# Weights of the first two experts asked for later, in an attention and mixture-of-experts kernel

## The chip, the cores and the metric

The kernel runs on one core of one Trainium2 chip, as one launch. The metric is device time in microseconds (us). TensorE (PE), VectorE (DVE), ScalarE (ACT) and GpSimd (POOL) each work through a list of instructions of their own, in order; SyncE (SP) issues most DMAs, GpSimd issues the indirect ones (gather and scatter by an index) and a few others. An instruction waits at the head of its engine's list until what it needs is there, and all that stands behind it waits too.

## What is computed

A gated linear attention over 4 sequences of 768 tokens with 8 heads of 40, and a mixture of 16 experts on its rows (3072 tokens, 320 wide, hidden size 1024). Cut to what matters:

```python
for t in range(S):                                   # attention, state C and n per sequence and head
    m_new = maximum(f[t] + m, i[t]); fs = exp(f[t] + m - m_new); is_ = exp(i[t] - m_new); m = m_new
    C = fs * C + is_ * outer(v[t], k[t]);  n = fs * n + is_ * k[t]
    y[t] = sigmoid(o[t]) * (C @ q[t]) / maximum(abs(n @ q[t]), 1)
x = y as rows of 320 (8 heads x 40)
g = argmax(x @ w_group)                              # one of 4 groups, then one of 4 experts in it
e = argmax(x @ w_expert[g])
out = softmax(..)[g] * softmax(..)[e] * (relu(x @ w1[g, e]) @ w2[g, e])
```

## The kernel before

**Attention.** The sequence is cut into 6 chunks of 128 tokens; a chunk of one of the 4 sequences is a unit, so there are 24 units, 0 to 23. A unit multiplies keys and queries (`sp`, line 200), weighs them with decays (`pt`, 205), adds what the carried state gives (`si`, 225) and multiplies with the values (`av`, 266). Its inputs are four kinds of DMA on SP: `ab` (the decays, 512 KB), `qk` (two of 192 KB), `nt` (values and keys, 324 KB), and every fourth unit `sig`. `ab` and `qk` of a unit are asked for four units ahead, `nt` three units ahead. Two units ahead GpSimd masks `ab` (`affine_select`, line 160) and ScalarE takes its exponential (190). For units below 20 GpSimd also scales the output rows (`hn`, 288), behind the mask in its list. The rows of the unit before (`x`, 293) are written to `x_d` in DRAM (301), transposed on TensorE (306) and multiplied with the routing weights (`lg`, 327).

**Routing.** `route()` (line 333 on) turns four units' logits into slots of an index table `itab` in DRAM. It is a generator: each small step, one to three instructions, is taken by `go_on()`, of which a unit has five; `go_on(7)` behind units 13 to 15 takes seven more. For the last two chunks it runs in two parts, over three units and over one. GpSimd scatters a unit's token numbers to `itab` (`put_id`, 455). At unit 13 `first_experts()` is put in the same list: from the counts so far it picks the two experts that go first, and its last steps put 8 tasks in `early_loads` (each asks for half of `w1`, 768 KB, or half of `w2`, 640 KB: for the first expert w1, w1, w2, w2, and then the same for the second) and 7 tasks in `early_splits`.

**Splits.** Weights are used as a sum of two rounded parts. A split task casts a piece on ScalarE (609) and lists the subtraction that gives the low part for VectorE (611, `lows`). The first expert has seven: w1, w1, a third piece `wsk`, and four quarters of w2.

**The turn from attention to experts.** Behind unit 22, when chunks 0 to 4 are routed, the last slots are scattered, the first expert's index list is read back (`ix`, 581), and 256 rows are gathered from `x_d` in two gathers (`xg`, 548). They are transposed (`tpm`, 646), split by ScalarE and VectorE (`xhl`, 653 and 654), and `expert((0, 0), 256)` starts (`psh`, 725; `po`, 758 to 760). Rows of the last chunk that belong to this expert come with a second, late gather of 128 rows. The other 15 experts follow one after the other, each with its weights loaded two experts ahead.

**What sets the order.** Units 2 to 21 are written out in the order in which they run (`manual_schedule`). From unit 22 on a planner places the instructions by its own costs; `issue_after` holds a block behind a given instruction and `high_priority` brings it forward. The stretch that the change touches:

```python
for u in range(2, MANUAL):                                     # MANUAL = 22
    unit(u)
    go_on(7 if 13 <= u <= 15 else 0)
    do(early_loads, 1 if 14 <= u < 20 else 0)
    do(lows)
    do(early_splits, {16: 1, 17: 1, 18: 2, 20: 2, 21: 1}.get(u, 0))
```

so that six halves are asked for behind units 14 to 19, one behind each, and the last two behind the last unit's write to `x_d`.

Of the kernel before, what the change touches and what calls it, by code (L numbers as in the profile page):

```python
# [7 lines left out]
F32 = mybir.dt.float32  # L8
# [4 lines left out]
ALU = mybir.AluOpType  # L13
# [5 lines left out]
P = 128  # L19
# [34 lines left out]
def bc(ap, shape):  # L54
    return ap.broadcast_to(list(shape))
# [3 lines left out]
def lstm_moe(ctx: ExitStack, tc: tile.TileContext, gates, qkT, nat, og, wcat, w1, w2, cst, out):  # L59
    nc = tc.nc  # L60
# [59 lines left out]
    rt = {"manual": True}  # L120


    def busy(n):
        t = ps_s.tile([P, 512], F32, name="busy", tag="sp")
        for _ in range(n):
            mm(t, ones_b, bc(ones_b.unsqueeze(1), (P, 4, P)), start=True, stop=True)
# [288 lines left out]
    def go_on(n=1):  # L415
        for _ in range(n):
            if chores:
                with ExitStack() as st:
                    if not rt["manual"]:
                        st.enter_context(tc.high_priority())  # L420
                    if next(chores[0], StopIteration) is StopIteration:
                        chores.pop(0)
# [28 lines left out]
    def put_id():  # L451
        if ids:
            sl, tk = ids.pop(0)
            nc.gpsimd.memset(sep, 0.0)
            no_order("ids", nc.gpsimd.indirect_dma_start(
                out=itab_flat, out_offset=bass.IndirectOffsetOnAxis(ap=sl, axis=0), in_=tk, in_offset=None))
# [120 lines left out]
    def load_ix(r, q=None):  # L577
        nb = len(blocks(CAPS[r]))
        ixs[r] = mxp.tile([P, 3, 2], I32, name="ix", bufs=5)
        t = itab[0:NE * NBLK].rearrange("(e n) p o -> e n p o", e=NE)  # L580
        (q or nc.sync).dma_start(ixs[r][:, 0:nb], t[bass.ds(ereg[r], 1), 0:nb].rearrange("o n p i -> p (o n) i"))

    def blocks(W):
        return [min(P, W - i) for i in range(0, W, P)]
# [15 lines left out]
    lows = []  # L600
# [33 lines left out]
    def turn_tasks(key, W, xg, banks=None):  # L634
        t = {}

        def one(i, m):
            if i == 0:
                pool = pools["xhl"][len(xhls) % len(pools["xhl"])]
                sh, dt = ([P, 3, W], F32) if key[0] in FULL else ([P, 3, 2, W], F32R)  # L640
                t["x"] = xhls[key] = pool.tile(sh, dt, name="xhl", bufs=1)
            xhl, g = t["x"], xg[i]
            pool, tag = (banks or ((ps_1, "tp"), (pools.get("ps_t"), "tg"), (ps_1, "av")))[i]
            tp = pool.tile([P, 3, P], F32, name="tpm", tag=tag)
            for k in range(3):
                nc.tensor.transpose(out=tp[:, k, :], in_=g[:, k * P:(k + 1) * P], identity=ident)  # L646
            if key[0] in FULL:
                nc.scalar.copy(xhl[:, :, i * P:i * P + m], tp[:, :, 0:m])

                nc.vector.memset(xhl[DM - 2 * P:, 2, i * P:i * P + m], 0.0)  # L650
                return
            xh = xhl[:, :, 0, i * P:i * P + m]
            nc.scalar.copy(xh, tp[:, :, 0:m])  # L653
            nc.vector.tensor_tensor(xhl[:, :, 1, i * P:i * P + m], tp[:, :, 0:m], xh.bitcast(F32), op=ALU.subtract)

        return [lambda i=i, m=m: one(i, m) for i, m in enumerate(blocks(W))]

# [129 lines left out]
    def do(tasks, n=99):  # L787
        while tasks and n:
            tasks.pop(0)()
            n -= 1  # L790

    def ix_of(r):
        return lambda i, m: ixs[r][0:m, i, :]

    xgs, early_loads, early_splits = {}, [], []
# [171 lines left out]
    with tc.manual_schedule():  # L967
        for u in range(2, MANUAL):
            unit(u)
            go_on(7 if 13 <= u <= 15 else 0)  # L970
            do(early_loads, 1 if 14 <= u < 20 else 0)
            do(lows)
            do(early_splits, {16: 1, 17: 1, 18: 2, 20: 2, 21: 1}.get(u, 0))
    rt["manual"] = False
    for u in range(MANUAL, NU + 1):
        unit(u)
        if u == 22:
            go_on(40)
            while ids:
                put_id()  # L980
            for r in range(NEARLY):
                load_ix(r, nc.gpsimd)
                xgs[r] = load_x(EARLY, ix_of(r), True)
            do(lows)
    with tc.issue_after(rt["xs"].ins):
        do(early_loads)
    do(early_splits)
    do(lows)
    logits(NU - 1)
    turns = turn_tasks((0, 0), EARLY, xgs[0], ((ps_a, "si"), (ps_s, "sp")))  # L990
    with tc.issue_after(rt["lg", NU - 1].ins), tc.high_priority():
        busy(8)
        do(turns)
    go_on(40)
    while ids:
        put_id()
# [27 lines left out]
    expert((0, 0), EARLY, wsp_[0], xgs[0], ix_of(0), last=turn_tasks((0, 1), LATE, xgs[0, 1]))  # L1024
    pools["late"] = True
    split = split_tasks(1)
    with tc.issue_after(rt["last"].ins):
        do(split, 3)
    expert((0, 1), LATE, wsp_[0], xgs[0, 1], late_ix[0], split, turn_tasks((1, 0), CAPS[1], xgs[1]))
    xgs[2] = load_x(CAPS[2], ix_of(2))  # L1030
# [24 lines left out]
    with tc.For_i(0, nv, 1):  # L1055
# [31 lines left out]
        tp = ps_1.tile([P, 3, P], F32, name="tpm", tag="tp")  # L1087
# [83 lines left out]
```

## Time and profile before

| what | value |
|---|---|
| median of 3 runs | 436.83 us (433.73 to 437.80) |
| the profiled execution, its own time | 431.86 us |
| its span, first to last instruction | 430.3 us |
| PE busy | 403.4 us, 94% of the span |
| DVE, ACT, POOL busy | 284.0, 239.7, 175.6 us |
| granted TensorE clock, mean | 0.96 of full speed |
| DMA | 97.06 MB, mean 226 GB/s |

TensorE is the busiest engine. The shares are means over two stages: attention until about 168 us, experts from 177 us on. A busy time on PE holds pipelined matmuls and says little about how fast they run: the granted clock has to be read with it. A wait is put down to what came last.

### The profile page before, as it was taken

The numbers are of one execution on the slowest core, as the hardware profiler recorded it, in microseconds if no ns is written. First come the engines' busy times: TensorE is split into PE (matmuls) and PEld (weight loads), VectorE is DVE, ScalarE is ACT, GpSimd is POOL, SyncE is SP. The second block draws the span as 40 slices with busy tenths as digits, with TensorE's granted clock in tenths as the row PEclk, the third lists the DMA queues.
The fourth block names the chain that finished last, engine by engine and source line by source line (L and its number), as shares of the span: only waits on it lengthen the run. The fifth ranks groups of instructions, "written<-read, shape, count | busy, mean of one in ns | idle before, by whom it ended". The sixth has DMA issues, their size and how long they took to land.

```text
span 430.3 us, 9707 instructions
## 1 busy us (share of the span) xinstructions
PE 403.4 (94%) x3587; PEld 378.3 (88%) x3587; DVE 284.0 (66%) x703; ACT 239.7 (56%) x566; POOL 175.6 (41%) x213
## 2 busy tenths in 40 slices
PE   7788899998999698699999999999999999999994
PEld 4677898987988686599999999999999999999994
DVE  5734786868589586766747585676585878767360
ACT  4457656664775443427637474575665666755251
POOL 1445566765763542355521406313214613322110
PEclk9689999998999689699999999999999999999998
DMA  5999999999999923268984646586578567531340
GB/s 167 297 311 315 306 315 283 312 262 266 298 299 304 274 60 104 95 188 298 424 321 161 205 150 216 166 291 224 200 244 286 217 214 265 201 138 36 133 167 11
DMA packets 29812, 97.06 MB, mean 226 GB/s; under 512 B 9681, under 2 KB 13402, under 8 KB 26180
## 3 DMA queue, kind: packets, MB, share of 16 engines
q1 hardware_dynamic: 24340, 79.46, 58.3%
q0 software_dynamic: 5152, 16.62, 11.4%
q8 instruction: 29, 0.48, 0.5%
q10 hardware_dynamic: 272, 0.36, 0.4%
q14 instruction: 19, 0.16, 0.1%
HBM read 86.85 MB, written 10.42 MB: 226 GB/s over the span
## 4 chain that ended last, share of the span: by engine, by line
PE 57%; issue 17%; DMA 9%; POOL 7%; DVE 5%; ACT 2%; POOLq 1%; SPq 0%; DVEq 0%
PE psh L725 21%; PE po L758 6%; PE po L759 6%; PE po L760 6%; PE av L266 3%; PE sp L200 3%; DMA ab<-a_d 3%; DMA qk<-in_qkT_dram 2%; DMA nt<-in_nat_dram 2%; PE tpm L646 2%; PE si L225 2%; POOL ab L160 2%; POOL out_dram L552 2%; DMA xg<-x_d,ix 2%; PE po L764 1%
## 5 line engine op out<-in xcount | busy, mean ns | idle before, releaser
L548 POOL DMA_INDIRECT xg<-x_d,ix x34 | 37.6, 1105 | 108.1 <-DMA ix<-itab 49.9
L190 ACT ACTIVATE ab<-ab,bcol 128x128 f32<-128x128 f32 x184 | 56.3, 388 | 24.1 <-POOL ab L160 23.7
L758 PE MATMUL po<-w2h,hh 128*128 128x320 f32 (+1 forms) x208 | 65.7, 316 | 0.0
L759 PE MATMUL po<-w2l,hh 128*128 128x320 f32 (+1 forms) x208 | 64.2, 309 | 0.0
L760 PE MATMUL po<-w2h,hh 128*128 128x320 f32 (+1 forms) x208 | 64.1, 308 | 0.0
L611 DVE TENSOR_TENSOR w2l<-w2s,w2h 128x640 fp32r<-128x640 f32 x64 | 50.1, 816 | 20.9 <-ACT w2h L609 20.7
L552 POOL DMA_INDIRECT out_dram<-y,ix x34 | 40.4, 1187 | 54.5 <-ACT y L770 36.7
L725 PE MATMUL psh<-xhl,w1h 128*128 128x256 f32 (+4 forms) x352 | 59.8, 291 | 0.6 <-ACT xhl L653 0.6
L266 PE MATMUL av<-nt,pt 128*128 128x128 f32 x384 | 55.4, 303 | 2.3 <-DVE pt L205 2.2
L266 PEld LDWEIGHTS av<-nt,pt 128*128 128x128 f32 x384 | 50.5, 211 | 3.9 <-DVE pt L205 2.7
L725 PEld LDWEIGHTS psh<-xhl,w1h 128*128 128x128 f32 x352 | 50.5, 193 | 1.5 <-ACT xhl L653 1.0
L679 ACT ACTIVATE hh<-psh 128x512 fp32r<-128x512 f32 (+5 forms) x60 | 29.9, 498 | 26.9 <-PE psh L725 22.8
L682 DVE SCALAR_TENSOR_TENSOR hh<-psh,hh 128x256 fp32r<-128x256 f32 (+2 forms) x88 | 35.1, 429 | 12.7 <-ACT hh L679 12.3
L609 ACT CAST w2h<-w2s 128x640 fp32r<-128x640 f32 x64 | 43.0, 725 | 0.7 <-DMA w2s<-in_w_dram 0.7
L205 DVE TENSOR_TENSOR pt<-sp,ab 128x512 f32<-128x512 f32 x48 | 31.8, 684 | 15.8 <-PE sp L200 15.6
L160 POOL TENSOR_SCALAR_AFFINE_SELECT ab<-ab 128x1024 f32<-128x1024 f32 (+1 forms) x25 | 26.9, 1076 | 34.4 <-DMA ab<-a_d 21.4
L611 DVE TENSOR_TENSOR w1l<-w1s,w1h 128x1024 fp32r<-128x1024 f32 x26 | 31.7, 1219 | 11.2 <-ACT w1h L609 8.9
L758 PEld LDWEIGHTS po<-w2h,hh 128*128 128x128 f32 (+1 forms) x208 | 38.9, 187 | 0.1
L759 PEld LDWEIGHTS po<-w2l,hh 128*128 128x128 f32 (+1 forms) x208 | 38.9, 187 | 0.0
L760 PEld LDWEIGHTS po<-w2h,hh 128*128 128x128 f32 (+1 forms) x208 | 38.8, 187 | 0.0
L770 ACT ACTIVATE y<-po,ix 128x320 f32<-128x320 f32 (+1 forms) x25 | 13.2, 528 | 43.1 <-PE po L760 40.9
L725 PE MATMUL psh<-xhl,wsk 128*128 128x256 f32 (+4 forms) x176 | 36.6, 290 | 0.0
(180 smaller groups left out, 831.6 us busy)
## 6 DMA issues: line engine op xcount, KB each, us to landing
w1s<-in_w_dram SPq DMA_DIRECT2D x12, 1536.0 KB, 7.5
w2s<-in_w_dram SPq DMA_DIRECT2D x12, 1280.0 KB, 6.9
ab<-a_d SPq DMA_DIRECT2D x23, 512.0 KB, 8.2
qk<-in_qkT_dram SPq DMA_DIRECT2D x48, 192.0 KB, 7.9
nt<-in_nat_dram SPq DMA_DIRECT2D x24, 324.0 KB, 6.8
x_d<-x SPq DMA_DIRECT2D x24, 192.0 KB, 6.5
sig<-in_og_dram SPq DMA_DIRECT2D x6, 640.0 KB, 6.1
w1s<-in_w_dram SPq DMA_DIRECT2D x4, 768.0 KB, 9.4
```

The lines of the kernel that those rows point to most:

```text
L160: nc.gpsimd.affine_select(out=a, in_=a, pattern=[[0, a.shape[1]], [1, P]], compare_op=ALU.is_ge, fill=fill, base=0, channel_multiplier=-1)
L190: rt["exp"] = nc.scalar.activation(ab[:, j, :], ab[:, j, :], AF.Exp, bias=bcol[:, c, b * H + j:b * H + j + 1])
L266: mm(av[:, o:o + P], t["pm"][j // 4][:, j % 4, :], nt[:, o:o + P], start=True, stop=True)
L548: return nc.gpsimd.indirect_dma_start(out=o, out_offset=None, in_=src, in_offset=bass.IndirectOffsetOnAxis(ap=idx, axis=0))
L552: return nc.gpsimd.indirect_dma_start(out=out, out_offset=bass.IndirectOffsetOnAxis(ap=idx, axis=0), in_=y, in_offset=None, bounds_check=N ...
L609: nc.scalar.copy(a, src[:, s])
L611: lows.append(lambda: nc.vector.tensor_tensor(o[rows], src[rows, s], a[rows].bitcast(F32), op=ALU.subtract))
L682: nc.vector.scalar_tensor_tensor(hh[:, f:f + per, dst], src[:, :, t], 0.0, hr.bitcast(F32)[:, :, t], op0=ALU.max, op1=ALU.subtract)
L725: ins = mm(ps[:, g * W:(g + 1) * W], w[:, s], x, start=(n == 0), stop=(n == len(todo) - 1))
L758: mm(po[0:m], hh[:, f, t], w2h[:, s], start=st0, stop=False)
L759: mm(po[0:m], hh[:, f, t], w2l[:, s], start=False, stop=False)
L760: ins = mm(po[0:m], hh[:, f, tl], w2h[:, s], start=False, stop=sp0)
```

## The change

The extra routing steps behind units 13 to 15 (seven each) become three behind each of units 13 to 16. The eight weight halves are asked for one behind unit 16, one behind 18, two behind 20, two behind 21, and the last two behind unit 22. The first expert's split tasks are taken behind units 18, 20 and 21 (the three of w1); its four w2 quarters are written behind the first expert's turned rows, whose last instruction is kept as `rt["xl"]`; the second expert's splits also go behind it. Between the two transposed row blocks stand four `busy` matmuls, which compute nothing that is used.

```diff
@@ turn_tasks
-            nc.vector.tensor_tensor(xhl[:, :, 1, i * P:i * P + m], tp[:, :, 0:m], xh.bitcast(F32), op=ALU.subtract)
+            ins = nc.vector.tensor_tensor(xhl[:, :, 1, i * P:i * P + m], tp[:, :, 0:m], xh.bitcast(F32), op=ALU.subtract)
+            if key == (0, 0):
+                rt["xl"] = ins
@@ units 2 to 21
-            go_on(7 if 13 <= u <= 15 else 0)
-            do(early_loads, 1 if 14 <= u < 20 else 0)
+            go_on(3 if 13 <= u <= 16 else 0)
+            do(early_loads, {16: 1, 18: 1, 20: 2, 21: 2}.get(u, 0))
             do(lows)
-            do(early_splits, {16: 1, 17: 1, 18: 2, 20: 2, 21: 1}.get(u, 0))
+            do(early_splits, {18: 1, 20: 1, 21: 1}.get(u, 0))
@@ units 22 to 24
         if u == 22:
+            do(early_loads)
             go_on(40)
@@ behind the units
-    with tc.issue_after(rt["xs"].ins):
-        do(early_loads)
-    do(early_splits)
-    do(lows)
     logits(NU - 1)
     turns = turn_tasks((0, 0), EARLY, xgs[0], ((ps_a, "si"), (ps_s, "sp")))
     with tc.issue_after(rt["lg", NU - 1].ins), tc.high_priority():
         busy(8)
+        do(turns, 1)
+        busy(4)
         do(turns)
+    with tc.issue_after(rt["xl"].ins):
+        do(early_splits)
+        do(lows)
@@ ahead of the first expert's late rows
-    with tc.issue_after(rt["last"].ins):
+    with tc.issue_after(rt["last"].ins), tc.issue_after(rt["xl"].ins):
         do(split, 3)
```

On SP, in the units 17 to 19 before, each unit's input requests (`nt`, `ab`, `qk`) stand behind a half of the weights (`w1s`, `w2s`; the `ISA` row sets the address from the chosen expert):

```order
L566 DMA w2s<-in_w_dram 128x1280
L176 DMA nt<-in_nat_dram 128x648
L167 DMA ab<-a_d 128x1024
L145 DMA qk_91<-in_qkT_dram 48x1024 x2
L301 DMA x_d<-x 128x384
L566 ISA
L566 DMA w1s<-in_w_dram 128x1536
L176 DMA nt<-in_nat_dram 128x648
L167 DMA ab<-a_d 128x1024
L145 DMA qk_92<-in_qkT_dram 48x1024 x2
```

With the change the same requests stand like this; the w1 half is the second and last one ahead of the attention's inputs:

```order
L167 DMA ab<-a_d 128x1024
L145 DMA qk_91<-in_qkT_dram 48x1024 x2
L301 DMA x_d<-x 128x384
L566 ISA
L566 DMA w1s<-in_w_dram 128x1536
L176 DMA nt<-in_nat_dram 128x648
L167 DMA ab<-a_d 128x1024
L145 DMA qk_92<-in_qkT_dram 48x1024 x2
L301 DMA x_d<-x 128x384
L176 DMA nt<-in_nat_dram 128x648
```

The other six halves follow between the last writes to `x_d`, where before five such writes stood without a weight between them.

On VectorE, at the start of the first expert (`xhl` is the first expert's rows, `hh` its hidden values, `big` and `pos` the choice of the other experts), the order before:

```order
L654 TENSOR_TENSOR xhl<-tpm,xhl 128x3x128 x2
L513 TENSOR_TENSOR big<-key 128x256
L611 TENSOR_TENSOR w1l<-w1s,w1h 128x1024
L515 TENSOR_REDUCE pos<-big 128x16
L611 TENSOR_TENSOR wsk<-w1s,wsk 64x1024
L519 TENSOR_TENSOR sel<-pos,cs 128x32
```

and with the change:

```order
L654 TENSOR_TENSOR xhl<-tpm,xhl 128x3x128
L611 TENSOR_TENSOR w2l<-w2s,w2h 128x640 x4
L521 TENSOR_TENSOR big<-sel,cs 128x32
L519 TENSOR_TENSOR sel<-pos,cs 128x192
L522 TENSOR_REDUCE eidr<-big 128x2
L528 TENSOR_TENSOR sel<-pos,cs 128x32
L521 TENSOR_TENSOR big<-sel,cs 128x192
L523 CAST ewi<-eidr 128x2
L684 SCALAR_TENSOR_TENSOR hh<-psh,hh 128x2x256
```

The four low parts of the first expert's w2 now stand directly behind its rows, ahead of its first hidden values (line 682 before, 684 now).

## Rows read from the trace of the kernel before

**Rows 1.** Timeline of PE: start us, us, work; scores of units 13 to 22, then the expert.

```profile
90.71 1.16 PE L200 MATMUL sp<-qk 40*128 40x128 f32 x16
...
105.93 1.16 PE L200 MATMUL sp<-qk 40*128 40x128 f32 x16
...
117.12 1.16 PE L200 MATMUL sp<-qk 40*128 40x128 f32 x16
...
135.03 1.16 PE L200 MATMUL sp<-qk 40*128 40x128 f32 x16
...
144.42 2.08 PE L200 MATMUL sp<-qk 40*128 40x128 f32 x16
...
153.73 1.16 PE L200 MATMUL sp<-qk 40*128 40x128 f32 x16
...
177.11 1.60 PE L725 MATMUL psh<-xhl,w1h 128*128 128x256 f32 x4 [0.57 <-ACT xhl L653]
```

**Rows 2.** Busy time by stretch: us, five engines, granted clock, DMA share, GB/s.

```profile
104.00:110.00 6.00, 6.00 (x72) 5.54 (x71) 3.71 (x15) 3.34 (x11) 3.67 (x7) 0.86 0.76 183
...
140.00:146.00 6.00, 2.66 (x20) 2.17 (x20) 1.37 (x7) 3.71 (x13) 4.23 (x8) 0.77 1.04 310
146.00:152.00 6.00, 6.00 (x44) 5.78 (x41) 5.29 (x21) 0.64 (x2) 2.58 (x10) 0.50 0.72 194
...
176.00:182.00 6.00, 5.42 (x29) 4.72 (x27) 4.83 (x12) 4.53 (x7) 0.94 (x1) 0.60 0.01 0
```

**Rows 3.** Timeline of POOL: start us, us, instruction [idle before it, and what ended it].

```profile
141.17 1.09 POOL L160 TENSOR_SCALAR_AFFINE_SELECT ab<-ab 128x1024 f32<-128x1024 f32 x1 [6.38 <-DMA ab<-a_d]
...
160.57 0.97 POOL L455 DMA_INDIRECT itab<-tokw,slot  x1 [4.68 <-DVE den L282]
163.90 0.80 POOL L581 DMA_DIRECT2D ix<-itab  x1 [2.36 <-DMA itab<-tokw,slot]
...
168.72 0.95 POOL L548 DMA_INDIRECT xg<-x_d,ix  x1 [0.30 <-issue]
```

**Rows 4.** Chain of waits: start us, us, what.

```profile
1.26 4.88 PE busy L126 x11
...
128.98 12.12 DMA ab<-a_d
...
168.72 6.81 DMA xg<-x_d,ix
```

**Rows 5.** Timelines of ACT (first row) and SP: start us, us, work.

```profile
157.24 0.23 ACT L300 COPY x<-x 128x64 f32<-128x64 f32 x1
...
145.59 22.50 SPq L301 DMA_DIRECT2D x_d<-x  x5
168.63 0.91 SPq L566 DMA_DIRECT2D w2s<-in_w_dram  x2
```

**Rows 6.** DMA issues: what, queue, operation, count, KB each, median us to landing.

```profile
ab<-a_d SPq DMA_DIRECT2D x23, 512.0 KB, 8.2
...
xg<-x_d,ix POOLq DMA_INDIRECT x34, 4.3
...
itab<-tokw,slot POOLq DMA_INDIRECT x24, 7.5
...
ix<-itab POOLq DMA_DIRECT2D x1, 3.0 KB, 3.2
```

**Rows 7.** Timeline of DVE: start us, us, instruction [idle before it].

```profile
160.14 0.15 DVE L407 TENSOR_TENSOR tokw<-sm,se 128x1 f32<-128x1 f32 x1
...
177.90 1.22 DVE L611 TENSOR_TENSOR w1l<-w1s,w1h 128x1024 fp32r<-128x1024 f32 x1
...
184.66 0.82 DVE L611 TENSOR_TENSOR w2l<-w2s,w2h 128x640 fp32r<-128x640 f32 x1
...
192.89 0.56 DVE L654 TENSOR_TENSOR xhl<-tpm,xhl 128x384 fp32r<-128x384 f32 x1 [2.70 <-ACT xhl L653]
```

**Rows 8.** Busy time of the experts' stretch, columns as in Rows 2.

```profile
177.00:430.00 253.00, 247.13 (x1835) 241.56 (x1835) 161.47 (x317) 141.59 (x267) 80.70 (x72) 0.99 0.58 202
```

## The prediction, made before the run

> **What bounds the kernel now.** I read the busy share by stretch first, then the chain of waits, then the timelines where the chain leaves TensorE. From 177 us on TensorE is busy 247.13 of 253.00 us at a granted clock of 0.99 [rows 8]: once the first expert starts, the rest follows at its own pace, and what moves that start moves the end. The start, at 177.11 [rows 1], hangs on two things: how fast the attention comes through, and the way from the routing of the last chunk but one to the gathered rows.
>
> In the attention a plain unit takes 5.60 us (units 15 and 16, 105.93 to 117.12, over two) [rows 1]. Two places are slower. Units 13 and 14 take 15.22 us together; behind them the DMA engines are no longer full (share 0.76, 183 GB/s) [rows 1, 2], so it is not the inputs that hold them up: it is the stretch with seven extra routing steps per unit. Units 20 and 21 take 18.70 us [rows 1]. There the chain runs over DMAs: the decays of unit 22 are 12.12 us under way, where the median is 8.2 [rows 4, 6]; GpSimd waits 6.38 us for them at its mask [rows 3]. Behind the mask in its list stand the scaled rows of the unit before, so TensorE's transposes wait too. TensorE is then busy 2.66 us of 6; the granted clock falls to 0.77 and to 0.50, its 1.2 GHz level, and the scores of unit 21 take 2.08 us for 1.16 [rows 1, 2]. The DMA engines are full while TensorE idles (share 1.04), and soon after they have little to do [rows 2].
>
> **The change part by part.**
>
> *Extra routing steps.* No step goes away; 21 extra slots behind three units become 12 behind four. Two plain units are 11.2 us, so units 13 and 14 hold 4.0 us too much. The steps still pass through VectorE, so all of it won't go: bounds 0 and -4.0. I take the middle, **-2.0**. The step that loads the experts' numbers into registers on SP and GpSimd moves one unit later with its wait and holds nothing new back.
>
> *Weight requests.* Of the halves that stood on SP ahead of the decays of unit 22 (w1, w1, w2, w2) one w1 is left; one more w1 stands behind them as before, and the w2 pair that followed is out of the attention's way. That takes 2,048 KB from ahead of those decays, 6.8 us at the 310 GB/s of the stretch [rows 2]. What has to vanish: two units at the pace of units 17 to 19 (17.91 over three, so 5.97) would take 11.9 us, against 18.70, so 6.8 us is lost there [rows 1]. The units also come 2.0 earlier now, so the inputs must come 6.4 + 2.0 us sooner; to the 6.8 I add the quarter of 6 us in which the engines idled [rows 2], 1.4: 8.2 against 8.4. So nearly all of the stall goes: **-6.2**, bounds -3.4 (half) and -6.8. If the cover fails, the decays of unit 23 are late next; but GpSimd reaches its mask for them long before TensorE wants them, so a small lateness there is free.
>
> *The way to the first rows.* From the last weight of the routed chunk (160.14) to the expert (177.11) are 16.97 us: scatter at 160.57, index load at 163.90, second gather at 168.72, which takes 6.81 us [rows 1, 3, 4, 7]. That gather now shares the engines with a pair of w2 halves issued at 168.63 [rows 5]; with the change these are gone by then, and a gather's median is 4.3 [rows 6]: -2.5, bounds 0 and -2.5. In exchange the second expert's four halves (2,816 KB, 9.3 us at 310 GB/s) leave behind the writes of units 20 and 21. Unit 20's row copy, which its write waits for, is at 157.24, 3.3 us ahead of the scatter [rows 3, 5], so the scatter meets the burst. Quiet, it had landed 3.3 us after its issue; the median of all 24, most of them with the engines full, is 7.5 [rows 3, 6]. Bounds 0 and +4.2; part of the burst lies ahead of it, so I take the middle, +2.1. The index load behind it, 3.2 us [rows 6], comes when the burst has some 2 us left: 0, at worst +5.0 (as the decays' 8.2). Together **-0.4**.
>
> The Trainium skill ("DMA: Bandwidth & Descriptors", section on queues, rings and completion order) says that a DMA engine takes turns between the queues that have work, a packet at a time, so that GpSimd's scatter would not stand behind SP's weights. By that rule the scatter stays at its quiet price and the sum is 2.1 us lower; no row here shows it, and the median of 7.5 speaks against it.
>
> *VectorE behind the first rows.* Four low parts of w2 at 0.82 us and one of w1 at 1.22 now come later, 4.5 us, ahead of the first hidden values and the late rows; before the late rows VectorE idles 2.70 us [rows 7]. The excess is 1.8 at most; some of the work on the expert choice now stands ahead of the rows, where VectorE waits anyway. **+0.6**, bounds 0 and +1.8. ScalarE's casts of these w2 quarters move into the last units, where it waits for TensorE's transposes: nothing; their cover gone, about what their low parts take, four times 0.82 us [rows 7].
>
> *Four `busy` matmuls* lie in the wait for the second gather: 0. If that wait were gone they would cost at most 1.8 us (eleven took 4.88 at the cold start [rows 4]). They may also keep the clock up; between 176 and 182 it is 0.60 [rows 2], so at full clock up to 2.4 us would come back. But the hidden values then meet VectorE's new order, so I take none of it.
>
> Sum: -2.0 - 6.2 - 0.4 + 0.6 = -8.0. The profiled execution took 431.86 us, 1.6 of it outside the span; so 423.9 by its count. The median of the runs is 436.83, 5.0 above it; taken from that, **428.8 us**.
>
> **Rivals.**
>
> *The hand-off is quiet* (chance 0.17). The scatter lands at 3.3 us in spite of the burst, and the clock is partly kept. For it: GpSimd's DMAs have a queue of their own. Against it: the 7.5. Then the sum is -10.1, with up to 2 us from the clock -12: 424.8 to 426.7. The rule of the Trainium skill named above would give this.
>
> *The change doesn't free the attention* (0.18). The engines are near full in the attention, and the window of requests on SP, not the weights, could set the pace; two halves are still ahead of unit 23. Against it: the 12.12 us come just where four halves have gone ahead. Then only the routing steps (-2.0) and the -0.4 stay, with +0.6 behind: some 435.
>
> *The burst covers the whole way* (0.08), the case on the slower side. Its place is the chain scatter, index load, gathers on GpSimd; each hop starts when the last has landed, so delays add. Price: +4.2 for the scatter, up to +8.9 for the index load (12.12 for 3.2), and +2.5 for a gather that loses its gain and meets twice the bytes: 15.6, against -8.2 in the attention and +0.6 behind: +8.0, 444.8; with half of the index load's price 440. It decides when the hops together lose over 8 us, which needs the 2,816 KB to last well over 10 us, under 275 GB/s. Against it: the engines moved 310 in a full stretch.
>
> *VectorE becomes the bound at the first expert* (0.07). The four low parts delay the first hidden values, these the third hidden group, and the late rows come behind all of it: 3.3 us of low parts and the 1.8 above, so the gain shrinks to about 3.5: 433.
>
> **How the numbers follow.** The forecast (chance 0.50) holds 426 to 432. The range of 8 in 10 runs from 421.5, where bounds of the routing steps and the quiet hand-off meet, to 436, where the attention isn't freed; left out are the slower case and the far ends. A change under 1%, 4.4 us, can't be told from none. Faster by more: the forecast but for its upper edge (0.46), the quiet hand-off (0.17), a little of the others (0.06): 0.69. Within 1%: 0.24, mostly the attention not freed and VectorE. Slower: 0.07.
>
> **What would show it.** In the changed kernel's profile the scores of units 20, 21 and 22 stand about 6 us apart and take 1.16 us, not 2.08; GpSimd's wait for the decays is under 1 us; the granted clock stays near 1.0 up to the last unit. Units 13 and 14 take 12 to 14 us together. The first `psh` starts at about 168.5. From the last scatter to the index load are 4 to 7 us, and the second gather lands in 4 to 5. The experts' stretch keeps its length within 1 us. I am wrong if the wait for the decays stays over 3 us (the stall wasn't the weights), if the hand-off takes over 20 us (the burst sits on it), or if TensorE waits for low parts or for the late rows in the first expert.

## The result, and the profile after

The changed kernel takes 427.91 us in the median of four runs (425.83 to 429.00), the kernel before 435.28 beside it (432.00 to 437.80). The ratio is 0.9876, 95% interval 0.9828 to 0.9924. Run again later beside other kernels (e5 below) the ratio was 0.9927, 0.9886 to 0.9968, at 428.05 us. So the change gives about 1%: 5.4 us by the one ratio, 3.2 by the other. (The ratios leave out untypically long executions, so they aren't the quotients of the medians.) The forecast was 428.8, in a range that ran from 421.5 to 436.0.

The profiled execution has a span of 425.8 us (430.3 before) at a mean granted clock of 0.964. 1.9 us of the 4.5 between the spans are there at unit 8, before anything has changed: its scores start at 60.21 for 62.12. Among the executions profiled here that start lies anywhere between 59.7 and 66.3. I therefore count from unit 8 on.

PE's timeline (start us, us, work) shows the scores of units 13, 15, 20, 21, 22 and 23 and the first expert:

```profile
88.84 1.16 PE L200 MATMUL sp<-qk 40*128 40x128 f32 x16
...
100.98 1.16 PE L200 MATMUL sp<-qk 40*128 40x128 f32 x16
...
130.00 1.16 PE L200 MATMUL sp<-qk 40*128 40x128 f32 x16
...
136.06 1.16 PE L200 MATMUL sp<-qk 40*128 40x128 f32 x16
...
141.15 1.16 PE L200 MATMUL sp<-qk 40*128 40x128 f32 x16
...
153.07 1.17 PE L200 MATMUL sp<-qk 40*128 40x128 f32 x15
...
173.53 1.23 PE L727 MATMUL psh<-xhl,w1h 128*128 128x256 f32 x4 [1.16 <-DVE xhl L654]
```

Beside [rows 1]: units 13 and 14 take 12.14 us (15.22 before), units 20 and 21 take 11.15 (18.70 before). All of the first gain is in unit 14 (8.93 before, 5.83 now; unit 13 is as long as it was). But unit 22, 6.89 before (its successor started at 160.62), now takes 11.92, and the first `psh` comes only 3.58 us earlier. The stretches around it, to be held against [rows 2] (us, the five engines, granted clock, DMA share, GB/s):

```profile
140.00:146.00 6.00, 4.68 (x58) 4.26 (x57) 5.96 (x26) 0.10 (x1) 3.86 (x4) 0.99 0.40 141
146.00:152.00 6.00, 4.86 (x21) 3.95 (x21) 4.36 (x21) 4.66 (x15) 0.96 (x1) 0.50 0.53 69
...
164.00:170.00 6.00, 1.10 (x9) 0.94 (x10) 0.85 (x11) 0.00 (x0) 3.26 (x4) 0.70 0.25 71
170.00:176.00 6.00, 4.84 (x19) 3.45 (x17) 4.64 (x11) 3.79 (x5) 2.57 (x3) 0.50 0.02 1
```

In 140 to 146 us VectorE is busy 5.96 of 6; behind that the clock is at 0.50, its 1.2 GHz level. From 164 on TensorE idles until the rows come. Where [rows 2] has DMA engines at 1.04 (310 GB/s) in 140 to 146, they now have a share of 0.40.

GpSimd's timeline, for [rows 3] (the last number is the idle time and what ended it):

```profile
131.28 1.09 POOL L160 TENSOR_SCALAR_AFFINE_SELECT ab<-ab 128x1024 f32<-128x1024 f32 x1 [1.91 <-DMA ab<-a_d]
...
141.72 1.77 POOL L455 DMA_INDIRECT itab<-tokw,slot  x1 [1.68 <-DVE eq L355]
143.80 0.95 POOL L455 DMA_INDIRECT itab<-tokw,slot  x1 [0.30 <-issue]
144.77 1.10 POOL L160 TENSOR_SCALAR_AFFINE_SELECT ab<-ab 128x1024 f32<-128x1024 f32 x1
...
152.00 0.96 POOL L455 DMA_INDIRECT itab<-tokw,slot  x1 [5.00 <-DVE den L282]
160.53 0.80 POOL L581 DMA_DIRECT2D ix<-itab  x1 [7.56 <-DMA x_d<-x]
165.82 1.00 POOL L548 DMA_INDIRECT xg<-x_d,ix  x1 [4.50 <-DMA ix<-itab]
167.13 0.95 POOL L548 DMA_INDIRECT xg<-x_d,ix  x1 [0.31 <-issue]
```

Before, the first gather stood at

```profile
167.42 1.00 POOL L548 DMA_INDIRECT xg<-x_d,ix  x1 [2.72 <-DMA ix<-itab]
```

The wait for the decays of unit 22 is 1.91 us, for 6.38. The mask for unit 23 (144.77) stands behind two scatters. From the last scatter to the index load are 8.53 us, for 3.33; from there to the first gather 5.29, for 3.52; from the second gather to `psh` 6.40, for 8.39. SP's timeline says what moves meanwhile, where [rows 5] has five row writes and then one w2 pair:

```profile
136.29 0.89 SPq L566 DMA_DIRECT2D w2s<-in_w_dram  x2
148.61 0.33 SPq L301 DMA_DIRECT2D x_d<-x  x1
149.14 0.86 SPq L566 DMA_DIRECT2D w1s<-in_w_dram  x2
150.09 0.38 SPq L301 DMA_DIRECT2D x_d<-x  x1
150.69 1.47 SPq L566 DMA_DIRECT2D w2s<-in_w_dram  x2
```

And VectorE's timeline has the last weights of the routed chunk, of three units and of one; the second of these is the one in [rows 7]:

```profile
141.28 0.16 DVE L407 TENSOR_TENSOR tokw<-sm,se 128x3 f32<-128x3 f32 x1
...
151.57 0.16 DVE L407 TENSOR_TENSOR tokw<-sm,se 128x1 f32<-128x1 f32 x1
```

The second expert's four halves, 2,816 KB, leave at 149 to 152, with the scatter at 152.00. The experts' stretch is as long as it was, here to be compared with [rows 8]:

```profile
174.00:425.00 251.00, 246.14 (x1835) 240.88 (x1834) 163.43 (x318) 142.03 (x267) 85.19 (x72) 0.99 0.58 204
```

One table holds what the profiled executions say: from the scores of unit 8 to the last weight of the routed chunk (`tokw`, 151.57), from there to the first `psh` (the hand-off), and from `psh` to the end.

| kernel | ratio to before (95%) | unit 8 to `tokw` | hand-off | `psh` to end |
|---|---|---|---|---|
| before | 1 | 98.02 | 16.97 | 253.19 |
| changed | 0.9876 (0.9828, 0.9924) | 91.36 | 21.96 | 252.27 |
| e1 six halves behind unit 20 | 0.9893 (0.9824, 0.9961) | 91.03 | 21.39 | 251.38 |
| e2 second expert's halves last | 0.9895 (0.9859, 0.9931) | 90.61 | 19.51 | 252.85 |
| e3 old routing steps | 0.9971 (0.9927, 1.0016) | 94.71 | 21.85 | 251.05 |
| e4 no busy matmuls | 0.9913 (0.9868, 0.9958) | 91.07 | 19.40 | 254.14 |
| e5 changed, again | 0.9927 (0.9886, 0.9968) | 90.77 | 18.99 | 254.09 |
| e6 mask first | 0.9931 (0.9883, 0.9980) | not read | | |
| e7 24 busy matmuls | 0.9967 (0.9930, 1.0005) | 90.49 | 17.96 | 257.18 |
| e8 w2 among the inputs | 0.9968 (0.9924, 1.0011) | 86.32 | 26.03 | 252.20 |
| e9 w1 early, w2 late, mask | 0.9988 (0.9943, 1.0034) | 90.72 | 22.35 | 254.28 |
| e10 halves between row writes, mask | 0.9952 (0.9919, 0.9985) | 95.72 | 19.90 | 254.70 |
| e11 the same, no mask | 1.0002 (0.9963, 1.0042) | 91.20 | 23.29 | 253.19 |
| e12 quiet hand-off, mask | 0.9865 (0.9804, 0.9925) | 88.98 | 18.44 | 254.23 |

A stage of one execution is uncertain by some 3 us: the changed kernel's own hand-off was 21.96 and 18.99. Each row is one execution, so a difference under that isn't told from chance. The medians of e6 to e12 are under their experiments; e6 is told by its time alone.

### The profile page after: what moved, and what is told of

Its sections match the earlier page's. It is cut to its first block, busy times and chain, and to the rows that moved or that the text cites. A ratio compares the mean times of both kernels' runs of the same rounds, so it can differ in the third digit from the quotient of the medians.

```text
span 425.8 us, 9713 instructions
## 1 busy us (share of the span) xinstructions
PE 400.4 (94%) x3591; PEld 374.5 (88%) x3591; DVE 283.4 (67%) x703; ACT 240.0 (56%) x566; POOL 180.9 (42%) x213
## 4 chain that ended last, share of the span: by engine, by line
PE 65%; issue 15%; DMA 6%; DVE 5%; POOL 5%; POOLq 1%; ACT 0%; SPq 0%; DVEq 0%
PE psh L727 21%; PE po L760 6%; PE po L761 6%; PE po L762 6%; PE av L266 5%; PE sp L200 4%; PE si L225 3%; PE tpm L646 3%; DMA a_d<-A__124 3%; PE lg L327 2%; PE po L766 2%; PE tp L306 2%; PE po L765 1%; POOL out_dram L552 1%; DMA nt<-in_nat_dram 1%
## 5 line engine op out<-in xcount | busy, mean ns | idle before, releaser
L548 POOL DMA_INDIRECT xg<-x_d,ix x34 | 41.9, 1233 | 110.2 <-DMA ix<-itab 44.5
L266 PE MATMUL av<-nt,pt 128*128 128x128 f32 x384 | 53.1, 294 | 1.1 <-DVE pt L205 1.0
L266 PEld LDWEIGHTS av<-nt,pt 128*128 128x128 f32 x384 | 48.4, 204 | 2.6 <-DVE pt L205 1.5
## 6 DMA issues: line engine op xcount, KB each, us to landing
w1s<-in_w_dram SPq DMA_DIRECT2D x4, 768.0 KB, 11.2
```

What stands on the lines that cost most here:

```text
L266: mm(av[:, o:o + P], t["pm"][j // 4][:, j % 4, :], nt[:, o:o + P], start=True, stop=True)
L548: return nc.gpsimd.indirect_dma_start(out=o, out_offset=None, in_=src, in_offset=bass.IndirectOffsetOnAxis(ap=idx, axis=0))
```

## The experiments

The first theory: the attention got faster as forecast, and the hand-off became longer because the second expert's weights meet the scatter and the index load. Rivals: the hand-off is long through the order on GpSimd and SP; what is gained comes from the routing steps alone.

**e1, all six remaining halves behind unit 20.**

```diff
-            do(early_loads, {16: 1, 18: 1, 20: 2, 21: 2}.get(u, 0))
+            do(early_loads, {16: 1, 18: 1, 20: 6}.get(u, 0))
```

> The changed kernel with all six remaining weight halves asked for behind unit 20 (2 behind 20, 2 behind 21 and 2 behind 22 before), so that they move while the engines idle between 140 and 152 us, ahead of the scatter. Theory (the second expert's burst makes the scatter and the index load slow): from the last weight of the routed chunk (tokw) to the first psh 17 to 18 us instead of 22.0, the scatter landing in 3 to 4 us instead of 8.2; the decays of unit 23 may come later, up to 2 us; time 3 to 5 us under the changed kernel's 427.9, 423 to 425. Rival (the hand-off is long through the order on GpSimd and SP, not through the burst): scatter to index load stays over 7 us, time 427 to 428. Rival (six halves at once hold up the inputs of units 22 and 23 as four did before): the stall moves to units 21 and 22, time 429 to 432.

Measured: 426.54 us, hand-off 21.39. The requests didn't come early: SP waited 3.8 us for decays in flight, and the second expert's halves left at 144.49 to 147.88, only some 4 us sooner. The index load came 7.70 us behind the scatter, still under the burst. So it tells the theory and the rival apart no further. It shows that asking earlier doesn't by itself make the burst end earlier: here the engines still moved 400 GB/s from 158 to 160 us, and the changed kernel's engines, asked later, were at work about as long.

**e2, the second expert's halves behind the last row write.** The six behind units 20 to 22 become two behind 20, and

```diff
+    with tc.issue_after(rt["xs"].ins):
+        do(early_loads)
```

as before the change.

> The changed kernel with the second expert's four halves put back behind the last row write, as before the change; the first expert's w2 pair stays behind unit 20. Theory (burst): scatter to index load back to 3.3 us from 8.5, index load to gather back to 3.5 from 5.3, the second gather again slow, 6 to 7 us for 3.0; hand-off 17 to 19 us; time 424 to 426. Rival (order, not burst): hand-off stays over 21 us, 427 to 428. Rival (unit 22's long stretch comes from the weights behind unit 21): unit 22 falls from 11.9 to under 8 us; the theory has it unchanged, since GpSimd's mask for unit 23 stands behind scatters that wait for VectorE.

Measured: 426.94 us. GpSimd's timeline, and TensorE's first transpose of the rows:

```profile
154.38 0.97 POOL L455 DMA_INDIRECT itab<-tokw,slot  x1 [5.00 <-DVE den L282]
158.13 0.81 POOL L581 DMA_DIRECT2D ix<-itab  x1 [2.78 <-DMA itab<-tokw,slot]
161.59 0.99 POOL L548 DMA_INDIRECT xg<-x_d,ix  x1 [2.65 <-DMA ix<-itab]
162.89 0.95 POOL L548 DMA_INDIRECT xg<-x_d,ix  x1 [0.30 <-issue]
```

```profile
168.82 0.48 PE L646 MATMUL tpm<-cs,xg 128*128 128x128 f32 x1 [4.19 <-DMA xg<-x_d,ix]
```

Scatter to index load is 3.75 us, index load to gather 3.46: with no weights under way both are back at the prices of before. The gathers now meet the weights (asked for at 161.46), and from the second gather to `psh` go 10.56 us. The burst theory holds for each hop; unit 22 stays at 10.26 us, so the weights aren't what makes it long. The time is that of the changed kernel: held against its two profiles, the burst costs the scatter and the index load 5 to 7 us in the one place, or the gathers 4 to 6 us in the other.

**e3, the old routing steps.**

```diff
-            go_on(3 if 13 <= u <= 16 else 0)
+            go_on(7 if 13 <= u <= 15 else 0)
```

> The changed kernel with the seven extra routing steps behind units 13 to 15 put back (three behind 13 to 16 in the change). Theory (the steps cost units 13 and 14 and what is saved there reaches the end): units 13 and 14 together 15 us instead of 12.1, every later time some 3 us later, 430 to 431. Rival (saved there, waited for later): units 13 and 14 slower, but units 20 to 22 shorter by as much, 427.5 to 428.5.

Measured: 430.55 us; e1, e2 and e4, run with it, have 426.54 to 428.52. Of 94.71 us to `tokw`, 3.4 to 3.9 more than in the two profiles of the changed kernel, 1.5 are a unit 12 that waited for late decays, which the steps can't have caused. Units 13 and 14 take 12.95 us, not 15. TensorE's wait in unit 14 is there, as a row of the kernel before and one of this kernel show:

```profile
101.31 2.95 PE L266 MATMUL av<-nt,pt 128*128 128x128 f32 x16 [1.82 <-DVE pt L205]
```

```profile
101.33 2.05 PE L266 MATMUL av<-nt,pt 128*128 128x128 f32 x16 [1.19 <-DVE pt L205]
```

Before, the wait for `pt` behind VectorE's routing steps was 1.82 us and the clock then fell to 0.54 (102 to 105 us), so that the values took 2.95 us; here it was 1.19 us and the clock stayed at 1.00. How much the steps cost depends on whether the clock falls. In this profile units 13 and 14 are only 0.8 us longer than in the changed kernel's first, and units 15 to 20 another 1.1. The stall of units 20 and 21 is gone here too (11.78 us), so it wasn't the steps that made it. By the ratios the steps are worth about 3 us (0.9971 against the mean of 0.9876 and 0.9927, on 432; some 2 us either way, from the intervals), the rest of the change 1.3 us (0.9971; from 3.2 faster to 0.7 slower), if the two simply add.

**e4, without the four busy matmuls.**

```diff
-        do(turns, 1)
-        busy(4)
         do(turns)
```

> The changed kernel without the four busy matmuls between the two transposed row blocks. Theory: they stand on the path, since the second gather lands about as they start: the first psh 1.0 to 1.8 us earlier, time 426 to 427. Rival (they keep the clock up): without them the granted clock of 170 to 182 us falls and the first expert's start costs the 1.5 us again or more, 428 to 430.

Measured: 428.52 us, ratio 0.9913, between the two of the changed kernel. The first `psh` starts 2.71 us behind the first transpose instead of 4.63:

```profile
169.15 0.47 PE L646 MATMUL tpm<-cs,xg 128*128 128x128 f32 x1 [4.32 <-DMA xg<-x_d,ix]
...
171.86 1.60 PE L727 MATMUL psh<-xhl,w1h 128*128 128x256 f32 x4 [0.57 <-ACT xhl L653]
```

`psh` to end is 254.14 us, 1.9 longer than in the first profile of the changed kernel and as long as in the second (e5), so what becomes of the gain isn't shown. The clock is at 0.50 from 170 to 176 both here and in the first profile, so the expert starts sooner, but at half speed. Neither theory: the four keep no clock, and a cost of theirs doesn't show in the time.

**e5, the changed kernel again**, the yardstick of e6 to e8.

> The changed kernel as it is, beside the other three on the same chip, as their yardstick: 0.987 to 0.991 of the time before, and the same places in the trace: units 20 and 21 some 11 us together, unit 22 10 to 12 us, hand-off (last weight of the routed chunk to the first psh) 21 to 22 us.

Measured: 428.05 us. Units 20 and 21 take 11.16 us, unit 22 11.05, scatter to index load 8.07, as before; the hand-off is 18.99, below what was expected: index load to gather took 4.21 us, and the clock was at 1.00 from 164 on. `psh` to end is 254.09, so of the 3.0 us 1.8 aren't there at the end.

**e6, GpSimd's mask for unit 23 ahead of the scatters.**

```diff
-        upper(ab, NEG)
+        ins = upper(ab, NEG)
+        if u == NU - 1:
+            rt["mask"] = ins
...
+                if "mask" in rt:
+                    st.enter_context(tc.issue_after(rt["mask"].ins))
```

> The changed kernel with GpSimd's mask for unit 23 ahead of the two table scatters that wait for VectorE's slots; their waits stay, only the order on GpSimd moves. Theory (unit 22 gives back 5 us because that mask, and with it ScalarE's exponential and the casts and copies behind it, stands behind the scatters): unit 22 takes 6 to 8 us instead of 10 to 12, the last weight of the routed chunk comes 3 to 4 us earlier, time 2 to 4 us under the changed kernel. Rival (unit 22 is long because VectorE brings the routing of the last chunk but one in one lump of some 6 us, whichever way GpSimd stands): unit 22 over 9.5 us, time within 1 us of the changed kernel.

Measured: 428.98 us, ratio 0.9931, as e5, which is what the rival says. In the later kernels with the same edit (e9, e10, e12) the two parts of the routing (`tokw` of three units, then of one) lie 7.8 to 8.4 us apart, for 10.3 in the changed kernel (141.28 to 151.57), so the mask did hold up the second part by 2 us; unit 22 still takes 9.5 to 11.2 us. The theory is right in the chain it names and wrong in its size. ScalarE's copy is no longer waited for, but VectorE still is, here in e12 for 2.21 us, where the changed kernel has 1.32:

```profile
150.26 0.17 PE L374 MATMUL lg<-oh,lt_b 128*128 128x16 bf16 x1 [2.21 <-DVE oh L366]
```

Behind it the clock is at 0.72 (152 to 158 us).

**e7, 24 busy matmuls ahead of the rows.**

```diff
-        busy(8)
-        do(turns, 1)
-        busy(4)
+        busy(24)
         do(turns)
```

> The changed kernel with 24 busy matmuls in one run ahead of the first transposed row block, in place of 8 there and 4 between the two blocks: they fill TensorE's wait for the gathered rows. Theory (the wait lets the granted clock fall to 0.50, and the first expert pays for it until about 177 us): clock 1.00 from 164 to 182, the first psh group of four 0.6 to 0.8 us long instead of 1.0 to 1.6, time 2 to 3 us under the changed kernel. Rival (the extra matmuls stand ahead of rows that have landed): the first transpose 1 us later, no gain, 0 to +1. Rival (the first expert is paced by VectorE's low parts and hidden values, not by TensorE): the clock is up and the time is the same.

Measured: 429.57 us, ratio 0.9967, not faster, rather slower than e5. The clock is 1.00 in every stretch from 146 to 182, and counted from unit 8 `psh` starts earlier (108.45 us) than in any run so far. But then:

```profile
186.03 0.55 PE L646 MATMUL tpm<-cs,xg 128*128 128x128 f32 x3 [4.08 <-DMA xg<-x_d,li]
```

```profile
182.73 1.00 POOL L548 DMA_INDIRECT xg<-x_d,li  x1 [11.63 <-DMA ix<-itab]
```

TensorE waits 4.08 us for the late rows, whose gather GpSimd issued at 182.73, counted from unit 8 2.9 us later than in the changed kernel. In this kernel's order the third expert's w1 request stands ahead of that gather in GpSimd's list, which it doesn't in the changed one. So the run doesn't settle what the clock alone is worth; it shows the next bound: TensorE comes to the late rows 13.5 us behind `psh`, and they come no sooner because it starts sooner.

**e8, the first expert's w2 pair among the inputs.**

```diff
-            do(early_loads, {16: 1, 18: 1, 20: 2, 21: 2}.get(u, 0))
+            do(early_loads, {16: 1, 17: 1, 18: 1, 19: 1, 21: 2}.get(u, 0))
```

> The changed kernel with the first expert's w2 pair back among the attention's inputs: one half behind each of units 16 to 19, as before from unit 16 on, 2 behind 21 and 2 behind 22 as in the change. Theory (1,280 KB more ahead of the decays of units 22 and 23 bring 4.1 us at 310 GB/s, of which the lead hides part): GpSimd's wait for the decays of unit 22 goes from 2 to 4 us or more, units 20 to 22 together 2 to 4 us longer, time 1 to 4 us over the changed kernel. Rival (what freed the attention is the splits that moved, or the routing steps, not the weights): the scores of units 20 to 22 stay where they are, within 0.5 us; time the same.

Measured: 430.33 us, ratio 0.9968, some 2 us over e5 with intervals that overlap, and not for the reason expected. GpSimd's wait for the decays of unit 22 is

```profile
132.91 1.09 POOL L160 TENSOR_SCALAR_AFFINE_SELECT ab<-ab 128x1024 f32<-128x1024 f32 x1 [3.48 <-DMA ab<-a_d]
```

3.48 us, for 1.91 and 1.97 in the two profiles of the changed kernel and 6.38 before; but the scores of units 20 to 22 stand where they stood (130.06, 136.13, 141.22). GpSimd's lead hides it: one more half ahead of the decays is free, the two more of before were not. So the scores came out as the rival says. It isn't thereby right: no run moves the splits alone, and here, too, two of the four halves that stood ahead of these decays before are out of their way. In this kernel's order the mask for unit 23 (140.40) stands ahead of the scatters too. The two `tokw` then lie 5.1 us apart and the last one comes 4 to 5 us earlier, but unit 22 still takes 11.76 us. The hand-off takes it all back, 26.03 us: the scatter leaves at 147.79, but the index load comes 12.44 us behind it. From unit 8 to `psh` this makes 112.35 us, between the changed kernel's 113.32 and 109.76; so the profiled execution, at 427.37 us one of the shortest of the ten, doesn't show where the median's 2 us are lost.

**e9, e10 and e11, halves placed behind the first expert's turned rows.** All three use

```diff
+    with tc.issue_after(rt["xl"].ins):
+        do(early_loads)
```

e9 for the second expert's w2 pair (its w1 pair behind unit 20), e10 and e11 for all four halves; e9 and e10 with the edit of e6 and without the four busy matmuls.

> The changed kernel without the four busy matmuls, GpSimd's mask for unit 23 ahead of the scatters, and the second expert's halves split: its w1 pair (1,536 KB) right behind the first expert's w2 pair behind unit 20, its w2 pair only behind the first expert's turned rows. Theory (the scatter lands when the burst of weights has gone through, whenever it was issued): the last weight of the routed chunk 2 to 4 us earlier by the mask, the scatter landed 3 to 5 us after its issue, the index load 3.2, gathers 3 to 4; hand-off 17 to 18 us; the experts' stretch 1 to 3 us longer, since the late rows and the second expert's weights come no sooner; time 3 to 5 us under the changed kernel, 0.978 to 0.983 of before. Rival (the w1 pair at unit 20 still covers the scatter, as in the run with six halves behind unit 20): hand-off over 20 us, 0.988 to 0.993. Rival (the second expert waits for its w2): an idle of TensorE of 3 us or more near 190, 0.99 to 1.00.

> The same, but all four halves of the second expert behind the first expert's turned rows: no weight moves from about 145 to 165. Theory: scatter to index load 3.3 to 3.8, index load to gather 3.5, second gather landed in 3 to 4 (7 where the weights were asked for at 161); first psh 5 us or more earlier than in the changed kernel, counted from unit 21; 2,816 KB then take some 7 to 9 us, and the second expert's splits come behind them, so that 2 to 4 us of it are lost about 190; 0.980 to 0.985 of before. Rival (nothing is lost there): 0.975 to 0.978. Rival (the second expert waits for its w1 and its splits): an idle of TensorE of 5 us or more, 0.99 to 1.00.

> The changed kernel with only the place of the second expert's four halves moved, behind the first expert's turned rows (the mask stays behind the scatters, the four busy matmuls stay). Theory: the last weight of the routed chunk where it is in the changed kernel; hand-off 17 to 18 us for 21 to 22 (scatter and index load quiet, gathers 3 to 4 us); the same loss about 190; 0.983 to 0.988 of before. Rival (the mask alone makes the difference between this run and the one with it): this run over 0.99 while the other is under 0.985.

Measured: 433.78, 432.27 and 434.20 us, ratios 0.9988, 0.9952 and 1.0002: the gain of the change is gone in e9 and e11 and half gone in e10 (by the ratios; the changed kernel wasn't run beside these three). The edit didn't do what it says. The halves were not held; they stand between the row writes in SP's list, as SP's and GpSimd's timelines of e11 show (`rt["xl"]` is an instruction of VectorE, where e2's `rt["xs"]`, which did hold them, is a DMA of SP):

```profile
156.05 0.32 SPq L301 DMA_DIRECT2D x_d<-x  x1
156.60 0.46 SPq L566 DMA_DIRECT2D w1s<-in_w_dram  x1
157.26 0.34 SPq L566 DMA_DIRECT2D w2s<-in_w_dram  x1
161.22 0.34 SPq L301 DMA_DIRECT2D x_d<-x  x1
```

```profile
154.66 0.97 POOL L455 DMA_INDIRECT itab<-tokw,slot  x1 [5.00 <-DVE den L282]
163.53 0.80 POOL L581 DMA_DIRECT2D ix<-itab  x1 [7.91 <-DMA x_d<-x]
169.83 1.00 POOL L548 DMA_INDIRECT xg<-x_d,ix  x1 [5.50 <-DMA ix<-itab]
```

Spread out like this, the weights meet every hop: 8.87 us from scatter to index load, 6.30 to the first gather, and a hand-off of 23.29. No rival had this; as tests of a late request the three are void. They are three more cases of the burst on the path, with hand-offs of 19.90 to 23.29 us. In e10 units 12 and 13 also took 18.05 us for 11.90, where GpSimd waited 4.63 us for decays and the clock fell to 0.50.

**e12, no weights near the hand-off.** e2 with the mask first and no busy matmuls.

> The changed kernel with the second expert's four halves behind the last row write (as in the second run), GpSimd's mask for unit 23 ahead of the scatters, and no busy matmuls between the row blocks: no weight is in SP's list between the w2 pair behind unit 20 and the last row write, so nothing that the runs so far found on the hand-off stays. In the three runs before, halves stood between the row writes in SP's list, so they met the scatter after all. Theory: scatter to index load 3.3 to 3.8 us, index load to first gather 3.5; the gathers are out before the weights and land in 3 to 4; first psh 3 us or more earlier than in the second run, counted from unit 21; part of it is lost at the late rows; 0.980 to 0.986 of before. Rival (what is gained up to the first expert is lost behind it, since the late rows and the second expert's weights come no sooner): psh as early, the experts' stretch longer by as much, 0.988 to 0.993.

Measured: 426.74 us, ratio 0.9865.

```profile
155.66 0.96 POOL L460 DMA_INDIRECT itab<-tokw,slot  x1 [2.78 <-DVE den L284]
161.88 0.80 POOL L586 DMA_DIRECT2D ix<-itab  x1 [5.26 <-DMA itab<-tokw,slot]
164.42 1.00 POOL L553 DMA_INDIRECT xg<-x_d,ix  x1 [1.74 <-DMA ix<-itab]
165.72 0.95 POOL L553 DMA_INDIRECT xg<-x_d,ix  x1 [0.30 <-issue]
```

```profile
152.00:158.00 6.00, 6.00 (x44) 5.14 (x44) 4.64 (x18) 2.39 (x6) 1.61 (x7) 0.72 0.13 41
158.00:164.00 6.00, 5.52 (x52) 4.73 (x50) 3.86 (x10) 1.70 (x4) 0.80 (x1) 1.00 0.12 36
```

The scatter to index load takes 6.22 us although the DMA engines are nearly idle (0.13 and 0.12), where 3.3 to 3.8 were expected; why the scatter lands so late there, no row shows. Index load to gather takes 2.54. The gathers don't get out ahead of the weights (164.47), and the second one's rows come after 6.8 us. Hand-off 18.44, `psh` to end 254.23. The ratio is just above what the theory gives and below the rival; from unit 21 to `psh` it is 32.32 us for 35.01 in e2, and 1.4 of these 2.7 are lost behind it. The interval (0.9804 to 0.9925) overlaps with both of the changed kernel's, so no version is shown to beat it.

## Why the prediction came true, and where its steps did not

The time was forecast within 1 us, and the direction with it, but that is partly luck: two errors cancel, a gain that was put too high and a starting point that was too high by about as much (see the sum).

**Routing steps: -2.0 said, about -3 measured.** The bounds held and the middle was too low: units 13 and 14 lost 3.1 of the 4.0 us that they had too much. VectorE is just as busy (5.86 of 6 us between 96 and 102, for 5.76 before), but TensorE's wait for `pt` in unit 14 is 0.36 us for 1.82, and the clock doesn't fall. By the times, undoing it (e3) costs 3 us, some 2 either way; so it is probably most of the gain, though e3's profile shows only 0.8 us of it in these units.

**Weight requests: -6.2 said.** The stall of units 20 and 21 went entirely, -7.55 us, beyond the bound of -6.8. That the weights had made it is not shown by a run of its own: e3 rules out the steps, the splits were never moved alone, and what speaks for the weights is that GpSimd's wait was one for a DMA and fell from 6.38 to 1.91 us. Yet the step failed in what it left out, "what is late next". I named the decays of unit 23 and held their lateness to be free. Late next was the routing of the last chunk but one. Before, its first part ended 3.2 us ahead of unit 22 (153.73):

```profile
150.56 0.16 DVE L407 TENSOR_TENSOR tokw<-sm,se 128x3 f32<-128x3 f32 x1
```

TensorE, which had gone through unit 21 at half its clock, then took unit 22 at full speed, with no wait above 0.2 us. Now that part ends at 141.28, as TensorE begins unit 22 (141.15), and TensorE waits twice, with ScalarE's part in it below:

```profile
144.09 0.17 PE L372 MATMUL lg<-oh,lt_b 128*128 128x16 bf16 x1 [1.32 <-DVE oh L364]
...
144.93 2.95 PE L266 MATMUL av<-nt,pt 128*128 128x128 f32 x16
149.01 1.65 PE L327 MATMUL lg<-wc,xT 128*128 128x128 f32 x6 [1.14 <-ACT xT L312]
```

```profile
145.90 2.44 ACT L190 ACTIVATE ab<-ab,bcol 128x128 f32<-128x128 f32 x8 [8.25 <-POOL ab L160]
```

The first wait is for a routing step on VectorE (`oh`). The second is for ScalarE's copy `xT`, which stands behind the exponential of unit 23's decays; for these ScalarE had waited 8.25 us, since their mask stands behind two scatters on GpSimd. So these decays weren't free, though not for want of a DMA. The waits make 2.5 of the 5.0 us that unit 22 is longer; the rest is work at the 0.50 clock behind them. In e2, at a clock of 1.00 throughout, the same two waits are 1.32 and 2.04 us, together just what unit 22 takes there (10.26) beyond the 6.89 of before. Net of unit 22, 2.5 us are left of 7.55. The wait for decays (1.91) is not under 1 us as said, and the clock did not stay near 1.0 until the last unit.

**Hand-off: -0.4 said, +5.0 and +2.0 in the two profiles.** In the first profile this is past the mark of 20 us that the prediction set itself as a sign of being wrong on the burst. The direction of the scatter's and the gather's terms was right, the sizes weren't. The scatter's +2.1 was the middle of 0 and +4.2, on the ground that part of the burst lies ahead of it; it measured +5.2 and +4.7, above the bound. The index load, taken as 0, cost +1.8 and +0.7. The gather's -2.5 came as -2.0 and -3.4. In the five profiles with the change's place for these halves (changed, e3, e4, e5, e7) the index load comes 7.0 to 8.8 us behind the end of the last w2 request, and in e8, where the scatter left 4 us earlier, 8.7: the scatter lands about when the burst has gone through, whenever it was issued. (Where the index load's row names a row write as what ended its wait, that only landed last; in the changed kernel the scatter itself landed 8.2 us behind its issue, and the index load came at 8.53. In e1 the last w2 request was out at 147.88 and the index load still came only at 159.47, but there the engines were busy with the burst until 160.) e2, which moves the burst alone, shows it to be the cause.

The rival of a quiet hand-off is thereby excluded. The Trainium skill ("DMA: Bandwidth & Descriptors", section on queues, rings and completion order) has each engine take turns between the queues that have work, packet by packet. The traces don't show that this guards a small scatter: from the scatter on GpSimd's queue to the index load it took 3.33 and 3.75 us without weights on SP's (before, e2) and 7.7 or more in each profile with them. The slower case, the burst on the whole way, came true in part: in e8 and e11, which are not the change, the hand-off is 9 and 6 us longer than before and most or all of the gain is gone, but the times (430.33 and 434.20) stay far from the 440 to 444.8 of that case.

**VectorE behind the first rows: +0.6 said.** `psh` to end is 252.27 and 254.09 us for 253.19 before; TensorE waits for no low part. Too small to be told.

**Busy matmuls: 0 said, none seen** (e4), but not for the reason given: they did lie on the path, 1.9 us of it up to `psh`. That the slow clock behind them made it no matter is likely and not shown.

**The sum.** Weights, splits and busy matmuls together were to bring 6.0 us; by e3 they bring 1.3 (from 3.2 faster to 0.7 slower). The steps bring about 3 for 2.0. So some 4 us for the 8.0. The median came out right because the forecast counts from 436.83, while the measured ratio puts the kernel before at 433.3 beside the changed one (427.91 / 0.9876): 3.5 us less, where the gain by that ratio, 5.4, is 2.6 less than said.

Open: why the scatter of e12 takes 6 us with idle engines; what moving the splits gives by itself; what the clock alone is worth at the first expert, since e7 moved an order too; and the decays that come late at unit 12 in some executions.

## What to carry to other kernels

A stall that vanishes on one engine uncovers the chain that ran under it: before counting it as a gain, look for what the other engines were doing in that time and when they finish. Bytes moved off one critical stretch land in another; here every place that was tried for 2,816 KB, between 144 and 167 us, cost some hop of a chain of small dependent transfers. And a wait of TensorE can cost more than it lasts when its clock falls behind it: 1.82 us in unit 14 before (clock 0.54 from 102 to 105 us) went with a unit 3.1 us longer.

## What was not expected of the hardware

- A small scatter is not protected by its own queue: 7.7 to 12.4 us to the load behind it under weight traffic, 3.3 to 6.2 without.
- In e1 the DMA engines have a mean share of 1.01 from 140 to 146 us and moved 119 GB/s; before, a share of 1.04 moved 310 in the same window. No run here explains it.
- TensorE idled 5 us behind 163.9 us and the clock was 0.50 from 170 to 176 us; filled with busy matmuls (e7) it was 1.00 throughout.
